# The product with w_out one step further behind the up products of a fused convolution and maxout FFN

## The chip, the cores and the metric

The kernel runs on one core of one Trainium2 chip. The metric is the time on the device in microseconds (us). Five engines work in parallel, each through its own list of instructions in order: TensorE (PE in the profile, its weight loads PEld), VectorE (DVE), ScalarE (ACT), GpSimd (POOL) and SyncE (SP, which issues DMAs here).

## The reference

Two blocks follow each other. The first is a long convolution by FFT with a filter that a small MLP makes, gated by x; the second is a maxout FFN with three up products.

```python
# x, v: (4, 12544, 128); pos_emb: (12544, 64)
h_filt = (np.maximum(pos_emb @ w1, 0.0) @ w2) * np.exp(-0.01 * pos)[:, None]
u = x * v
y = np.fft.irfft(np.fft.rfft(u, n=2 * S, axis=1) * np.fft.rfft(h_filt, n=2 * S, axis=0)[None],
                 n=2 * S, axis=1)[:, :S, :]
t = (x * y).reshape(50176, 128)
h = np.maximum(np.maximum(t @ moe_w1, t @ moe_w2), t @ moe_w3)   # d_ff = 768
out = h @ moe_w_out
```

## The kernel before

**The FFN.** Work goes by tiles of 392 tokens: 32 tiles in each of four batches, and six blocks f of 128 hidden channels in each tile. w1 was subtracted from w2 and w3 beforehand and w1 @ w_out folded into one matrix lin, so that a block needs only two up products: `up` (L674) makes `pa` with four matmuls, ScalarE takes the ReLU into `hid` (L679), four matmuls make `pb`, and VectorE takes the maximum of `hid` and `pb` (L682). `down` (L685) adds the block's product with w_out to the tile's sum in PSUM, the tile `ops`. With the first block it also adds lin times the tile, and with the last one ScalarE copies the sum to `ot` (L695) and GpSimd issues the DMA to the output (L697). All matmuls of `pa`, `pb`, `ops` and `yps` are recorded at L154, the helper `halves_mm`; they are told apart by tile.

**The tile's input.** `t_load` (L619) fetches the convolution's third-stage result `zt` from a scratch in HBM and the tile of x. `t_sums` (L643) makes the sum and the difference of its two halves: on GpSimd (L647, L648) in the first batch and in the first half of the others, on VectorE with a sign (L651) otherwise. `t_last` (L655) does the last stage of the inverse transform, 32 small matmuls into `yps`, and VectorE multiplies it with x into `gt` (L669).

**What runs beside it.** The FFN of batches 0, 1 and 2 shares the engines with the convolution of the next batch. `conv_steps` (L572) spreads that over the 192 steps (32 tiles x 6 blocks) of a batch, by a schedule written out by hand. First come the first-stage transforms `u_first` (L399: L408 on TensorE, L417 on ScalarE, L419 on VectorE). In the second half of a batch come pairs of frequencies: `g_quarter` (L452: L462, L472 on TensorE into `psq`), `g_fold` (L484 on ScalarE, two L487 on VectorE), `q_swap` (L502, L503, twice each, on ScalarE), `q_re` (L507), `q_im` (L512 on VectorE, L515 on GpSimd), `q_unfold` (two L520 on VectorE) and `g_store` (L495, a DMA from GpSimd).

**The order.** Each engine executes its instructions in the order in which the program issues them. The loop at L1015 issues, in step (tile, f): loads and, at f = 1, the sums of the next tile; `up` of this step; `down` of an earlier step; at f = 3 `t_last` of the next tile; then the convolution's work of this step. In the last tile of a batch the sums and `t_last` stand one or two steps later. After 96 tiles the loop ends with the first `up` of the last batch (L1048) and what is left of `down`; the last batch runs in another loop, without a convolution beside it, and products of its own (L742).

**The buffers.** `hid` has three (the default of `up`), the PSUM pool `hps` for `pa` and `pb` together three, which are taken in turn; `yps`, `ps1` and `psq` share two (`cps`), and `ops` has one.

```python
h = up((b, i), f)
if late is not None:
    down(*late)
late = ((b, i), f, h)
```

Of the kernel before, what the change touches and what calls it, by code (L numbers as in the profile page):

```python
# [89 lines left out]
def kernel(  # L90
# [59 lines left out]
    def halves_mm(out, lhsT, rhs, start, stop):  # L150


        for h in range(2):
            nc.tensor.matmul(out[64 * h:64 * h + 64], lhsT[:, 64 * h:64 * h + 64], rhs,  # L154
                             start=start, stop=stop, skip_group_check=True)
# [416 lines left out]
    def conv_steps(b, done):  # L572


        out = []

        def at(slot, late, fn, *args):
            out.append((slot, late, len(out), fn, args))

        per_pair = 170 / (NK + LATE + 0.6 * (NU - done))
        for u in range(done, NU):
            s = (u - done) * 0.6 * per_pair + 9
            at(max(0, int(s) - 9), 0, u_load, b, u)
            at(int(s) - 6, 0, u_mul, u)
            at(int(s) - 5, 0, u_planes, u)
            at(int(s) - 4, 0, u_dma, u)
            at(int(s), 0, u_join, u)
            at(int(s + 1), 1, u_first, u)  # L590
        s0 = int((NU - done - 1) * 0.6 * per_pair + 9) + 6
        for x in range(NK + LATE):
            s = s0 + int(x * per_pair)
            g, z = x if x < NK else None, x - LATE if x >= LATE else None
            at(s, 1, g_quarter, g, z)
            at(s + 1, 0, g_fold, g, z)
            at(s - 4, 0, w_load, x)
            if z is not None:
                at(s + 3, 0, g_store, b, z)
            if g is None:  # L600
                continue
            if g % 2 == 0:
                at(s - 4, 0, q_load, g, min(2, NK - g))
                at(s - 1, 0, h_load, g, min(2, NK - g))
            at(s + 2, 0, q_swap, g)
            at(s + 3, 0, q_re, g)
            at(s + 4, 0, q_im, g)
            at(s + 6, 0, q_unfold, g)
        slots = {}
        for s, _, _, fn, args in sorted(out, key=lambda r: r[:3]):  # L610
            slots.setdefault(s, []).append((fn, args))
        return slots
# [6 lines left out]
    def t_load(b, i):  # L619
        zt = hp.tile([N1, 2, 512], FP32, tag="zt", name="zt", bufs=2)  # L620
        for c in range(2):
            if b == 0:
                nc.sync.dma_start(
                    zt[NK * c:NK * c + NK],
                    zd[b].rearrange("(g a) c t f -> g a c t f", a=2)[
                        :, :, c, 2 * i:2 * i + 2, :].rearrange("g a t f -> g a (t f)"))
                continue
            q, j = divmod(i, NT // 2)
            for a in range(2):
                nc.sync.dma_start(  # L630
                    zt[NK * c:NK * c + NK, a].rearrange("g (t f) -> g t f", t=2),
                    zd[b].rearrange("(g a) c t q f -> g a c t q f", a=2)[
                        :, a, c ^ (a & q), 2 * j:2 * j + 2, q, :])
        zts[b, i] = zt[:, 0], zt[:, 1]
        if i % 2:
            return
        xT = hp.tile([D, 2, 4, NB], FP32, tag="xT", name="xT", bufs=2)
        for c in range(GC):
            nc.sync.dma_start(xT[c * NG:(c + 1) * NG].rearrange("d i p n -> d (i p) n"),
                              x[:, 4 * i:4 * i + 8, c, b, :])  # L640
        xTs[b, i], xTs[b, i + 1] = xT[:, 0], xT[:, 1]

    def t_sums(i, eng=nc.gpsimd):  # L643
        z0, z1 = zts[i]
        even = hp.tile([N1, 512], FP32, tag="even", name="even", bufs=2)
        if i[0] == 0 or i[1] < NT // 2:
            eng.tensor_tensor(out=even[:], in0=z0, in1=z1, op=ALU.add)  # L647
            eng.tensor_tensor(out=z1, in0=z0, in1=z1, op=ALU.subtract)  # L648
        else:
            for out, op in ((even[:], ALU.add), (z1, ALU.subtract)):  # L650
                nc.vector.scalar_tensor_tensor(out=out, in0=z1, scalar=sign_t[:, 0:1], in1=z0,  # L651
                                               op0=ALU.mult, op1=op)
        zts[i] = even[:], z1

    def t_last(i):  # L655
        zt = zts.pop(i)
        ps = cps.tile([P, state["yps"]], FP32, tag="cv", name="yps")
        own = i[0] == B - 1 and i[1] > 1
        g = (lp if own else hp).tile([D, 4, NB], FP32, tag="g", name="gt", bufs=4 if own else 3)
        y = ps[:, 0:N].rearrange("d (p n) -> d p n", p=4)  # L660

        h = NB // 2
        for s in range(4):
            for a in range(2):
                halves_mm(y[:, s, a * h:a * h + h], zt[a][:, s * D:(s + 1) * D],
                          f4p[:, i[0] > 0 and i[1] >= NT // 2, a, :], s == 0 and a == 0, True)
        y = y.rearrange("d p (a m) -> d p m a", a=2)
        xT = xTs.pop(i)
        nc.vector.tensor_tensor(out=g[:].rearrange("d p (m a) -> d p m a", a=2), in0=y,  # L669
                                in1=xT.rearrange("d p (m a) -> d p m a", a=2),  # L670
                                op=ALU.mult)
        gs[i] = g

    def up(i, f, tag="hid", bufs=3):  # L674
        rhs = gs[i][:].rearrange("d p n -> d (p n)")
        h = (lp if tag[0] == "h" and tag != "hid" else hp).tile([P, N], FP32, tag=tag, name="hid", bufs=bufs)
        pa = hps.tile([P, 512], FP32, tag="hps", name="pa")
        halves_mm(pa[:, 0:N], w_sb[1][:, f * P:(f + 1) * P], rhs, True, True)
        nc.scalar.activation(h[:], pa[:, 0:N], Relu)  # L679
        pb = hps.tile([P, 512], FP32, tag="hps", name="pb")  # L680
        halves_mm(pb[:, 0:N], w_sb[2][:, f * P:(f + 1) * P], rhs, True, True)
        nc.vector.tensor_tensor(out=h[:], in0=h[:], in1=pb[:, 0:N], op=ALU.max)  # L682
        return h

    def down(i, f, h):  # L685
        if f == 0:
            pos_[i] = ops.tile([D, 512], FP32, tag="ops", name="ops")
            halves_mm(pos_[i][:, 0:N], lin[:], gs[i][:].rearrange("d p n -> d (p n)"), True,
                      False)
        halves_mm(pos_[i][:, 0:N], wo_sb[:, f, :], h[:], False, f == NF - 1)  # L690
        if f < NF - 1:
            return
        gs.pop(i)
        o = op_.tile([D, 4, NB], FP32, tag="o", name="ot")
        nc.scalar.copy(o[:].rearrange("d p n -> d (p n)"), pos_.pop(i)[:, 0:N])  # L695
        dst = outT.rearrange("d (p b n) -> d p b n", b=B, n=NB)[:, 4 * i[1]:4 * i[1] + 4, i[0], :]
        nc.gpsimd.dma_start(dst, o[:])  # L697
# [94 lines left out]
    def run(steps):  # L792
        for fn, args in steps:
            fn(*args)
# [216 lines left out]

    tiles = [(b, i) for b in range(B) for i in range(NT)]
    LAST = (B - 1) * NT
    late = None
    for n, (b, i) in enumerate(tiles[:LAST]):  # L1015
        if i == 0:
            beside = {}
            beside = conv_steps(b + 1, EARLY if b == 0 else 0)
        if n == 0:
            t_load(*tiles[0])  # L1020
            t_load(*tiles[1])
            t_sums(tiles[0], nc.vector)
            t_last(tiles[0])
        for f in range(NF):

            if i < NT - 2:
                if f == 0:
                    t_load(*tiles[n + 2])
            elif i == NT - 1 and f < 2 and n + 1 + f < len(tiles):
                t_load(*tiles[n + 1 + f])  # L1030
            turn_ = i == NT - 1
            if f == (3 if turn_ else 1):
                t_sums(tiles[n + 1], nc.vector if turn_ else nc.gpsimd)
            if f == 4 and n + 1 == LAST:
                t_sums(tiles[n + 2], nc.vector)
            h = up((b, i), f)
            if late is not None:
                down(*late)
            late = ((b, i), f, h)
            if f == (4 if turn_ else 3):  # L1040
                t_last(tiles[n + 1])
            if f == 5 and n + 1 == LAST:
                t_last(tiles[n + 2])
            s = i * NF + f
            run(beside.pop(s, ()))
            if s == NT * NF - 1:
                assert not beside, sorted(beside)
    first = up((B - 1, 0), 0)  # L1048
    down(*late)
    conv.close()  # L1050


# [20 lines left out]
    step, b = 0, B - 1  # L1073
    for i in range(0, NT, 2):
        h = {}
# [63 lines left out]
```

## Time and profile before

The median of three runs is 2386.82 us (2385.32 to 2388.51). The profiled execution spans 2387.4 us, at a mean granted TensorE clock of 0.993.

| engine | busy us | share of the span | instructions |
|---|---|---|---|
| TensorE | 2318.9 | 97% | 27853 |
| its weight loads | 1367.3 | 57% | 27853 |
| VectorE | 1514.4 | 63% | 2798 |
| ScalarE | 1165.6 | 49% | 2124 |
| GpSimd | 976.0 | 41% | 1153 |

The changed loop runs from about 336 us (first matmul into `ops`) to 1961 us. In a line of a group, the engine and the operation are followed by the tiles written and read, the shapes and the count, then busy us and mean ns of one instruction, and after the bar the idle time of the engine just before these instructions, with what ended most of it. A line of the timeline gives start, duration, engine, line, operation, tiles and, in brackets, the idle time before it and its releaser. The ends of matmuls are modelled: the 0.83 us shown for a group of four run 0.17 us into the next group, which starts 0.66 us after it. A line of the table by stretches gives the stretch, its length, then busy us and count of TensorE, weight loads, VectorE, ScalarE and GpSimd, the granted clock, the share of time that the DMA engines were busy, and GB/s.

### The profile page before, as it was taken

How to read it: one execution, taken by the hardware profiler on the slowest of the kernel's cores; microseconds unless marked ns; L12 is line 12 of the kernel's file. 1: busy time of each engine (PE TensorE's matmuls, PEld its weight loads, DVE VectorE, ACT ScalarE, POOL GpSimd, SP SyncE). 2: the span in 40 equal slices, each digit the busy share in tenths (PEclk: the TensorE clock that was granted, in tenths of full speed). 3: DMA queues.
4: the chain of work that ended last, by engine and by line, in shares of the span. 5: the costliest groups of instructions: out<-in, count | busy, mean ns of one | idle time of the engine just before them, and what ended most of it. 6: DMA issues, size and time to landing. Idle time of an engine off the chain costs nothing.

```text
span 2387.4 us, 67988 instructions
## 1 busy us (share of the span) xinstructions
PE 2318.9 (97%) x27853; PEld 1367.3 (57%) x27853; DVE 1514.4 (63%) x2798; ACT 1165.6 (49%) x2124; POOL 976.0 (41%) x1153
## 2 busy tenths in 40 slices
PE   8999989999999999999999999999999999999998
PEld 7989856654444446654444446654444445666665
DVE  5578857756666647756777747756777755444543
ACT  2688844456556524446565524445556532222222
POOL 1045423334444434424333324434233315666666
PEclk9999999999999999999999999999999999999999
DMA  6878959798988669969889849969989832222221
GB/s 153 200 211 268 285 145 190 151 205 223 221 227 215 172 130 191 186 148 248 207 223 242 201 111 194 184 141 238 223 214 239 222 90 57 69 53 57 71 57 22
DMA packets 473145, 410.92 MB, mean 172 GB/s; under 512 B 328004, under 2 KB 374231, under 8 KB 472834
## 3 DMA queue, kind: packets, MB, share of 16 engines
q1 hardware_dynamic: 433504, 317.61, 60.0%
q0 software_dynamic: 26400, 75.72, 11.0%
q10 hardware_dynamic: 12930, 13.25, 1.7%
q8 instruction: 219, 3.59, 0.7%
q14 instruction: 92, 0.75, 0.1%
HBM read 262.77 MB, written 84.67 MB: 146 GB/s over the span
## 4 chain that ended last, share of the span: by engine, by line
PE 79%; ACT 6%; DVE 6%; DMA 4%; issue 4%; ACTq 0%; POOL 0%; SPq 0%; DVEq 0%; POOLq 0%
PE pa L154 19%; PE pb L154 18%; PE ops L154 16%; PE ops L742 6%; PE ps L408 5%; PE yps L154 5%; PE psq L462 3%; PE ps L163 3%; PE psq L472 2%; DVE cb L487 2%; ACT xs L503 1%; ACT xs L502 1%; DMA hd<-ht 1%; ACT ht L934 1%; DVE hid L682 1%
## 5 line engine op out<-in xcount | busy, mean ns | idle before, releaser
L682 DVE TENSOR_TENSOR hid<-hid,pb 128x392 f32<-128x392 f32 x768 | 428.0, 557 | 564.1 <-PE pb L154 295.7
L679 ACT ACTIVATE hid<-pa 128x392 f32<-128x392 f32 x768 | 383.9, 500 | 640.6 <-PE pa L154 624.9
L154 PE MATMUL pb<-gt,w_sb 128*64 128x392 f32 x3072 | 641.4, 495 | 7.8 <-ACT hid L679 7.8
L154 PE MATMUL pa<-gt,w_sb 128*64 128x392 f32 x3072 | 648.1, 499 | 0.8 <-DVE gt L669 0.8
L154 PE MATMUL ops<-hid,wo_sb 128*64 128x392 f32 x2304 | 481.9, 496 | 30.8 <-DVE hid L682 29.9
L154 PEld LDWEIGHTS pb<-gt,w_sb 128*64 128x64 f32 x3072 | 218.4, 137 | 305.1 <-issue 250.8
L515 POOL TENSOR_TENSOR cb<-cb,xs 128x512 f32<-128x512 f32 x135 | 174.5, 1293 | 466.5 <-DVE xs L512 229.3
L154 PEld LDWEIGHTS ops<-hid,wo_sb 128*64 128x64 f32 x2304 | 160.9, 136 | 261.1 <-issue 147.4
L154 PEld LDWEIGHTS pa<-gt,w_sb 128*64 128x64 f32 x3072 | 196.2, 137 | 137.8 <-issue 93.2
L502 ACT ACTIVATE xs<-cb 32x512 f32<-32x512 f32 x270 | 169.4, 628 | 205.7 <-DVE cb L487 203.2
L697 POOL DMA_DIRECT2D out_dram<-ot x96 | 74.7, 778 | 435.9 <-ACT ot L695 344.1
L419 DVE TENSOR_TENSOR spec<-ps,high 128x360 f32<-128x360 f32 (+1 forms) x204 | 141.9, 737 | 117.2 <-ACT high L417 116.9
L487 DVE TENSOR_TENSOR cb<-psq,eo 128x512 f32<-128x512 f32 (+1 forms) x288 | 174.6, 646 | 0.0
L503 ACT COPY xs<-cb 32x512 f32<-32x512 f32 x270 | 166.2, 616 | 3.2
L417 ACT COPY high<-ps 128x360 f32<-128x360 f32 (+1 forms) x102 | 77.3, 762 | 170.9 <-PE ps L408 113.3
L408 PEld LDWEIGHTS ps<-f1q,uT 98*64 98x64 f32 x3072 | 132.4, 137 | 34.7 <-issue 31.8
L154 PEld LDWEIGHTS yps<-f4p,even 90*64 90x64 f32 x2048 | 117.7, 140 | 41.7 <-issue 36.5
L408 PE MATMUL ps<-f1q,uT 98*64 98x90 f32 x3072 | 137.0, 241 | 3.1 <-DVE spec L419 2.6
L154 PE MATMUL yps<-f4p,even 90*64 90x49 f32 x2048 | 127.2, 222 | 3.5 <-DMA f4p<-f4p_const 3.5
L154 PE MATMUL yps<-f4p,zt 90*64 90x49 f32 x2048 | 128.8, 224 | 0.1
L669 DVE TENSOR_TENSOR gt<-yps,xT 128x392 f32<-128x392 f32 x128 | 72.1, 563 | 84.5 <-PE yps L154 42.3
L520 DVE TENSOR_TENSOR xs<-cb 128x256 f32<-128x256 f32 x270 | 120.4, 487 | 0.0
(130 smaller groups left out, 3336.1 us busy)
## 6 DMA issues: line engine op xcount, KB each, us to landing
ht<-hd SPq DMA_DIRECT2D x264, 256.0 KB, 5.8
wt<-wq_const SPq DMA_DIRECT2D x144, 256.0 KB, 6.4
zd<-cb POOLq DMA_DIRECT2D x135, 256.0 KB, 5.6
zt<-zd SPq DMA_DIRECT2D x384, 90.0 KB, 3.1
sq<-spec SPq DMA_DIRECT2D x264, 128.0 KB, 6.8
ut<-in_xr_dram SPq DMA_DIRECT2D x128, 196.0 KB, 4.1
ut<-in_vr_dram SPq DMA_DIRECT2D x128, 196.0 KB, 4.3
xT<-in_x_dram SPq DMA_DIRECT2D x256, 98.0 KB, 3.7
```

Source lines behind the costliest of these rows:

```text
L154: nc.tensor.matmul(out[64 * h:64 * h + 64], lhsT[:, 64 * h:64 * h + 64], rhs, start=start, stop=stop, skip_group_check=True)
L408: nc.tensor.matmul(ps[64 * c:64 * c + 64, 256 * i + h * N1:256 * i + (h + 1) * N1], t[:, 2 * ((at + i) % 8) + h].rearrange("n r t -> n (r ...
L417: nc.scalar.copy(high, v[:, 0])
L419: nc.vector.tensor_tensor(out=spec[:, :, a, at:at + n], in0=v[:, 1], in1=high, op=op)
L487: nc.vector.tensor_tensor(out=cb[:, a, lo:hi], in0=ps[:, lo:hi], in1=eo[:, lo:hi], op=op)
L502: nc.scalar.mul(xs[at:at + 32], xt[at + 32:at + 64], -1.0)
L503: nc.scalar.copy(xs[at + 32:at + 64], xt[at:at + 32])
L515: nc.gpsimd.tensor_tensor(out=xts[g], in0=xts[g], in1=xs[:], op=ALU.add)
L520: nc.vector.tensor_tensor(out=ab[:, q], in0=y[:, 0], in1=y[:, 1], op=op)
L679: nc.scalar.activation(h[:], pa[:, 0:N], Relu)
L682: nc.vector.tensor_tensor(out=h[:], in0=h[:], in1=pb[:, 0:N], op=ALU.max)
L742: nc.tensor.matmul(ps[64 * c:64 * c + 64, 0:H2], w, rhs[:, H2 * c:H2 * c + H2], start=start, stop=True, skip_group_check=True)
```

## The change

In the loop over the first three batches `down` lags two steps behind `up` in place of one: the maximum of a block is made two steps before TensorE multiplies it with w_out. It is meant to give VectorE more time to make that maximum before TensorE needs it. The last two downs follow the first `up` of the last batch. The number of buffers and every instruction stay as they are.

```diff
-    late = None
+    late = []
     for n, (b, i) in enumerate(tiles[:LAST]):
...
             h = up((b, i), f)
-            if late is not None:
-                down(*late)
-            late = ((b, i), f, h)
+            late.append(((b, i), f, h))
+            if len(late) > 2:
+                down(*late.pop(0))
             if f == (4 if turn_ else 3):
                 t_last(tiles[n + 1])
...
     first = up((B - 1, 0), 0)
-    down(*late)
+    for l in late:
+        down(*l)
     conv.close()
```

## The prediction

> **What bounds the kernel now.** I read the page first. TensorE is busy 97% of 2387.4 us, VectorE 63%, ScalarE 49%, and the granted clock is 0.99, so the kernel can gain only where TensorE stands still. The groups of instructions say where (busy and mean ns | idle before, and what ended it):
>
> ```profile
> L154 PE MATMUL pb<-gt,w_sb 128*64 128x392 f32 x3072 | 641.4, 495 | 7.8 <-ACT hid L679 7.8
> L154 PE MATMUL ops<-hid,wo_sb 128*64 128x392 f32 x2304 | 481.9, 496 | 30.8 <-DVE hid L682 29.9
> ```
>
> The product with w_out (down, tile ops) carries 30.8 us of TensorE's idle time, nearly all of it a wait for the max of L682; the second up product (pb) carries 7.8 us, a wait for the ReLU of L679. The waits of TensorE alone give counts and the longest single wait:
>
> ```profile
> PE ops L154 <- DVE hid L682: 29.9, 28, 2.0
> PE pb L154 <- ACT hid L679: 7.8, 11, 3.7
> ```
>
> Only 28 of the 576 downs in question are late, by about 1.07 us each. The longest pb wait, 3.73 us at 1967.09, stands outside the changed loop's steady part. The table by stretches (first columns: stretch, length, TensorE busy) shows where the rest lies:
>
> ```profile
> 536.00:830.00 294.00, 284.99 (x3096) 141.95 (x3094) 194.95 (x356) 173.99 (x317) 135.80 (x131) 0.99 0.84 215
> 830.00:1075.00 245.00, 245.00 (x2774) 138.16 (x2770) 151.40 (x264) 103.55 (x190) 90.15 (x113) 1.00 0.84 162
> 1075.00:1380.00 305.00, 292.01 (x3204) 140.53 (x3204) 219.12 (x405) 180.34 (x330) 103.04 (x107) 1.00 0.89 221
> 1620.00:1925.00 305.00, 292.06 (x3200) 140.14 (x3194) 217.85 (x401) 181.55 (x332) 103.71 (x108) 1.00 0.91 222
> ```
>
> While the first half of a batch runs (830 to 1075) TensorE never stops. It stops where g_quarter, g_fold and q_swap run beside the FFN: 9.0 us in the first such stretch, 13.0 and 12.9 us in the next two. That is the whole prize, 34.9 us, and about 0.2 us more for each wait (below). The timeline of TensorE shows one late down, which recurs nearly alike eight times (1132, 1185, 1271, 1323 and again in the last stretch):
>
> ```profile
> 1130.02 0.83 PE L154 MATMUL pb<-gt,w_sb 128*64 128x392 f32 x4
> 1132.31 0.88 PE L154 MATMUL ops<-hid,wo_sb 128*64 128x392 f32 x4 [1.47 <-DVE hid L682]
> 1133.12 0.67 PE L462 MATMUL psq<-sq,wt 64*64 64x128 f32 x16
> ...
> 1134.15 0.88 PE L154 MATMUL pa<-gt,w_sb 128*64 128x392 f32 x4
> 1134.86 0.83 PE L154 MATMUL pb<-gt,w_sb 128*64 128x392 f32 x4
> ```
>
> From pb's start to that of the down pass 2.29 us, where 0.66 is usual (1129.36 to 1130.02): 1.63 us lost, with 1.47 recorded as idle, and the group behind starts 0.15 us later than usual (0.81 after the down), elsewhere 0.05. VectorE and ScalarE at the same place:
>
> ```profile
> 1131.70 0.55 DVE L682 TENSOR_TENSOR hid<-hid,pb 128x392 f32<-128x392 f32 x1
> ```
> ```profile
> 1130.44 0.63 ACT L502 ACTIVATE xs<-cb 32x512 f32<-32x512 f32 x1 [1.89 <-DVE cb L487]
> ...
> 1132.34 0.61 ACT L503 COPY xs<-cb 32x512 f32<-32x512 f32 x1
> 1132.98 0.50 ACT L679 ACTIVATE hid<-pa 128x392 f32<-128x392 f32 x1
> ```
>
> The max comes late because L520, L507, L487 and the two L651 stand ahead of it in VectorE's order; the next ReLU comes late because four swaps stand ahead of it on ScalarE. The first is what the change attacks. The second is not touched.
>
> **What the Trainium skill says.** "TensorE: Matmul & The Clock Gate", Part 3, The mechanism: matmuls start and end in program order. The trace agrees: during the 1.47 us the queued L462 does not overtake. So what counts is what stands ahead of which wait. "Perfetto Trace Analysis", Optimization Strategy: the same gap repeating on the engine that should be saturated can mean too few buffers. The trace half agrees: the gaps repeat, and the pb waits are such a wait for a PSUM buffer. "SBUF — State Buffer", Who interferes with whom: a VectorE instruction with two SBUF inputs and a GpSimd one that reads SBUF exclude each other. The trace agrees: two L520, 0.75 us together at 1127.79, take 3.58 us beside the sums of L647 and L648:
>
> ```profile
> 572.04 3.58 DVE L520 TENSOR_TENSOR xs<-cb 128x256 f32<-128x256 f32 x2
> ```
> ```profile
> 571.12 0.79 POOL L697 DMA_DIRECT2D out_dram<-ot  x1 [1.33 <-ACT ot L695]
> 571.91 0.71 POOL L495 DMA_DIRECT2D zd<-cb  x1
> 572.51 1.40 POOL L647 TENSOR_TENSOR even<-zt 90x512 f32<-90x512 f32 x1
> ```
>
> **The change, part by part.** No instruction is added or removed; every down moves one step later in TensorE's order.
>
> The hid buffers. Three exist, and with the longer lag three are live: the ReLU of step n overwrites the buffer that down(n-3) read. On TensorE down(n-3) now stands just ahead of pa(n), and the ReLU must wait for pa(n) anyway. Cost 0, hidden by pa (0.66 us).
>
> The wait for the max. hps has three buffers in turn, so pa(n+2) needs the buffer that max(n) frees, and pb(n+1) the one that ReLU(n) frees. Until now down(n) met max(n) first. Now pa(n+2) does, later by one down (0.66 us) and the convolution's matmuls of that step (0 to 2 us). The late max is then mostly covered. The pb wait keeps its place, and TensorE reaches it sooner: this decides what is left of the prize.
>
> Site kind B, the one shown, eight times. After pb (1130.02 + 0.66) TensorE does the older down until 1131.34, then L462 and L472 (1.03 us, from 1133.12 to 1134.15) until 1132.37; max is done at 1132.25, so pa runs at 1132.37 instead of 1134.15. Then pb must wait for the ReLU, which ends at 1133.48: it starts at about 1133.53 instead of 1134.86, and pays about 0.2 us of restart. Net 1.1 us of the 1.47. The 0.46 us pb wait that follows some 11 us later (1143.54) hangs on a chain that itself starts from TensorE's yps, so it moves along and stays. 8 x 1.1 = 8.8 us.
>
> Site kind C (1.15 us at 1089.30, six times). The same walk: the next ReLU ends only at 1091.92, behind four swaps, and pb started at 1091.97 already. Net 0, between -0.2 and +0.5 each.
>
> Small downs (0.08 to 0.57 us, 2.3 us over the two last stretches): half kept, 1.1 us.
>
> Site kind A (1.95 us, four times in the first stretch, each with one of 0.30). The walk at 577.94 gives: pa could run at 578.45, but the ReLU ends at 580.55, so pb starts at 580.60 instead of 581.41, net 0.6 us after the restart; the ScalarE-bound stretch behind it (swaps until 594.01 and 602.74) then takes about as much back. Net 0, between -0.4 and +0.6.
>
> Moved along: the copy ot (L695) and the output DMA (L697), with their down. On GpSimd L697 waits for ot, and the sums of L647/L648 queue behind it. With the longer lag the last down of a tile falls into step 1 of the next, and the sums are issued ahead of that step's down: they no longer queue behind L697. Here 1.33 us of idle and 0.79 us of L697 go from ahead of them, and they start about 2 us earlier, beside L507 and L682 instead of two L520. Of the 2.83 us of exclusion (3.58 - 0.75) I expect about 1.3 us to remain, so 1.5 us less on VectorE. That chain (L520, L512, L487, swaps, ReLU) is what then binds pb, so some 0.6 us of it counts, between -0.5 and 1.2. Four sites: 2.4 us. What queues behind L697 in its new place, L515 and the stores, has 4 to 7 us of idle before it at these sites.
>
> The end of the loop. Before the first up of the last batch one down fewer has been done, and two follow it in place of one. The last down, its copy, the output DMA and the ReLU that waited for it until 1966.54 come at the same distance: 0. The last stretch, from 1961 us on, is unchanged: 0.
>
> Sum: 8.8 + 0 + 1.1 + 0 + 2.4 = 12.3 us, less about 1.3 us for new short ReLU waits where TensorE had been late enough to see none: 11 us. 2386.8 - 11 = 2375.8 us.
>
> **The rivals.** *All late downs are covered and nothing takes their place*: 29.9 us and 28 restarts of 0.2 us, so 35 us, 2352 us. For it speaks that VectorE and ScalarE are busy only 72% and 60% in the worst stretches; against it the walks above, in which a ReLU bounds pb three times out of three. *The wait moves one for one* from the max to the ReLU: 2386 us, no change. For it speaks kind C; against it kind B, where 1.3 us lie between the ReLU's end and the old pb. *Slower*: the sums, now earlier on GpSimd, meet L507, L512 or L520 in tiles where they met nothing. Some 15 tiles of the first convolution stretch can each lose up to 1.3 us of VectorE (one L647), 20 us; if three quarters of it shows on TensorE, 15 us, less the 9.9 us of B and the small downs, that is +5 us, 2392 us. Against it: VectorE is busy only 66% there, and the worst overlap exists already.
>
> **How the numbers follow.** My forecast, a gain of about 5 to 17 us: 0.76; all covered: 0.07; one for one: 0.12; slower: 0.05. The low end takes B at 1.4, C at 0.4, A with the sums at 1.2 and the small downs in full: 11.2 + 2.4 + 4.8 = 18 us, 2368.5. The high end takes B at 0.7 and nothing else, with A at -0.4: 5.6 - 1.6 = 4 us, 2383. Faster by over 0.2% (4.8 us): 0.82; within: 0.13; slower: 0.05.
>
> **What would show it.** After the change the idle time ahead of ops should fall from 30.8 to under 3 us, and that ahead of pb rise from 7.8 to 20 to 30 us with ACT hid L679 as releaser; pa should hardly wait for DVE hid L682. TensorE's idle time in the three stretches should fall from 34.9 to about 25 us, in the last two most. The two L520 of kind A should take less than 3.58 us. Wrong would be: pa waits for the max (slack too small), ReLU waiting for ops (hid buffers too few), or pb idle growing by as much as ops idle falls.

## The result and the profile after

The changed kernel takes 2375.54 us (median; 2374.38 to 2377.9) beside 2386.09 us for the kernel before (2385.32 to 2388.51): a ratio of 0.9955 [0.9938, 0.9973]. That is a gain of 10.6 us, where 11 were forecast. The number is right; the experiments show that the sum behind it isn't. One term of it was too small by some 9 us, and losses of some 7 us were put at nothing.

The groups of instructions of the changed kernel, for the same two groups (busy us and mean ns | idle before, and what ended it):

```profile
L154 PE MATMUL pb<-gt,w_sb 128*64 128x392 f32 x3072 | 644.9, 497 | 33.3 <-ACT hid L679 33.3
L154 PE MATMUL ops<-hid,wo_sb 128*64 128x392 f32 x2304 | 478.5, 492 | 0.0
```

The down no longer waits at all, and the second up product waits 33.3 us for the ReLU, where it waited 7.8. Together 38.6 us of idle time became 33.3. That is half of the gain; the other half shows as TensorE's busy time, which fell from 2318.9 to 2312.2 us with the same 27853 instructions. A part of that is the clock (next section), the rest was not followed. The waits of TensorE give the count:

```profile
PE pb L154 <- ACT hid L679: 33.3, 53, 3.7
```

There were 11 such waits before; now there are 53. No wait of `pa` for the max shows (its 0.8 us belongs to `gt`). The same four stretches as before (first columns: stretch, length, TensorE busy; the last is shifted by 10 us, since the program is ahead by then):

```profile
536.00:830.00 294.00, 288.75 (x3160) 142.58 (x3158) 192.06 (x366) 177.64 (x325) 138.61 (x135) 1.00 0.90 220
830.00:1075.00 245.00, 243.65 (x2762) 138.20 (x2760) 146.08 (x258) 103.83 (x188) 87.03 (x113) 1.00 0.84 163
1075.00:1380.00 305.00, 294.55 (x3266) 144.98 (x3264) 221.03 (x414) 180.75 (x332) 102.93 (x107) 1.00 0.90 219
1610.00:1915.00 305.00, 294.73 (x3268) 145.10 (x3264) 221.40 (x412) 183.40 (x336) 104.25 (x108) 1.00 0.92 223
```

TensorE's idle time is 5.25, 10.45 and 10.27 us in the first, third and fourth row: 26.0 us in place of 34.9. And the stretch in which it never stopped now has 1.35 us of idle time. The site of kind B that the prediction walked through, on TensorE:

```profile
1125.97 0.83 PE L154 MATMUL pb<-gt,w_sb 128*64 128x392 f32 x4
1126.63 0.83 PE L154 MATMUL ops<-gt,lin 128*64 128x392 f32 x4
1127.29 0.83 PE L154 MATMUL ops<-hid,wo_sb 128*64 128x392 f32 x4
...
1129.08 0.88 PE L154 MATMUL pa<-gt,w_sb 128*64 128x392 f32 x4
1130.15 0.88 PE L154 MATMUL pb<-gt,w_sb 128*64 128x392 f32 x4 [0.19 <-ACT hid L679]
```

and on VectorE and ScalarE:

```profile
1128.32 0.55 DVE L682 TENSOR_TENSOR hid<-hid,pb 128x392 f32<-128x392 f32 x1
```
```profile
1128.96 0.61 ACT L503 COPY xs<-cb 32x512 f32<-32x512 f32 x1
1129.60 0.91 ACT L679 ACTIVATE hid<-pa 128x392 f32<-128x392 f32 x2
```

The max of the first `pb` ends at 1128.87, later than the down behind that `pb` starts (1127.29). It makes nobody wait now, because that down uses an older block. What binds the next `pb` is the first of the two ReLUs at 1129.60, which had to wait for four swaps on ScalarE. From `pb` to `pb` it is 4.18 us here with 0.66 us of a lin product in between, so 3.52; before it was 4.84 (1130.02 to 1134.86). The gain is 1.32 us, and the walk gave 1.33 before the restart.

### The profile page after: what moved, and what is told of

It is laid out like the page before. It is cut to its first block, busy times and chain, and to the rows that moved or that the text cites. A ratio compares the mean times of both kernels' runs of the same rounds, so it can differ in the third digit from the quotient of the medians.

```text
span 2376.1 us, 68062 instructions
## 1 busy us (share of the span) xinstructions
PE 2312.2 (97%) x27853; PEld 1372.2 (58%) x27853; DVE 1489.2 (63%) x2798; ACT 1165.4 (49%) x2124; POOL 968.7 (41%) x1153
## 3 DMA queue, kind: packets, MB, share of 16 engines
q8 instruction: 219, 3.59, 0.7%
## 4 chain that ended last, share of the span: by engine, by line
PE 78%; ACT 8%; DMA 5%; DVE 4%; issue 3%; ACTq 0%; POOL 0%; SPq 0%; DVEq 0%; POOLq 0%
PE pb L154 19%; PE pa L154 19%; PE ops L154 16%; PE ops L742 6%; PE ps L408 5%; PE yps L154 5%; PE ps L163 3%; PE psq L462 2%; ACT xs L503 2%; ACT xs L502 2%; DMA hd<-ht 2%; DVE cb L487 2%; PE psq L472 2%; ACT hid L679 1%; ACT ht L934 1%
## 5 line engine op out<-in xcount | busy, mean ns | idle before, releaser
L154 PE MATMUL pb<-gt,w_sb 128*64 128x392 f32 x3072 | 644.9, 497 | 33.3 <-ACT hid L679 33.3
L154 PEld LDWEIGHTS ops<-hid,wo_sb 128*64 128x64 f32 x2304 | 168.8, 137 | 210.4 <-issue 210.4
L697 POOL DMA_DIRECT2D out_dram<-ot x96 | 75.1, 783 | 323.1 <-ACT ot L695 285.5
L503 ACT COPY xs<-cb 32x512 f32<-32x512 f32 x270 | 166.2, 616 | 3.1
L377 POOL COPY planes<-ut 128x784 uint16<-128x784 uint16 x90 | 75.9, 843 | 135.6 <-DVE ut L356 135.4
```

Source lines behind the costliest of these rows:

```text
L377: nc.gpsimd.tensor_copy(pl_[:, :, :, 0:NB], a[:].bitcast(U16).rearrange("p s (n h) -> p h s n", h=2))
L503: nc.scalar.copy(xs[at + 32:at + 64], xt[at:at + 32])
```

## Where the time went, stretch by stretch

One mark recurs in every kernel: the start of the ReLU of the first block of a tile. From the differences between such marks comes the gain of each stretch against the kernel before, in us. "(1, 10)" is tile 10 of batch 1; the columns are the changed kernel and three of the experiments below.

| from – to | time before | changed kernel | output DMA later, lag 1 | lag 2, PSUM in strict turn | and swaps split |
|---|---|---|---|---|---|
| (0, 0) – (0, 10) | 170.1 | -2.30 | -0.89 | +0.67 | +0.41 |
| (0, 10) – (0, 30) | 336.2 | +7.45 | +8.39 | +7.44 | +15.68 |
| (0, 30) – (1, 10) | 201.9 | -2.00 | -0.01 | -0.34 | -0.35 |
| (1, 10) – (1, 30) | 343.7 | +6.36 | +1.93 | +5.64 | +17.09 |
| (1, 30) – (2, 10) | 201.9 | -1.96 | -0.01 | -0.37 | -0.36 |
| (2, 10) – (2, 30) | 344.3 | +7.18 | +2.24 | +7.19 | +15.62 |
| (2, 30) – end | 455.8 | -1.52 | -0.12 | -1.10 | -0.87 |
| sum | | 13.21 | 11.53 | 19.13 | 47.22 |

The profiled span fell by 11.3 us (2387.4 to 2376.1). The remaining 1.9 us of the 13.2 lie ahead of the loop: the profiled run of the changed kernel reached the first mark at 335.45 us and that of the kernel before at 333.53, with the same program up to there. Over all runs that mark lies between 331.2 and 335.9 us, so differences of one or two microseconds between single spans mean nothing. Differences between marks inside the loop do mean something, where the clock is the same.

It isn't the same everywhere. In the kernel before, two stretches of 3.41 us, from 646.0 and from 782.5 us, have half the clock. They follow two of the four longest late downs; behind the other two, with a wait just as long, the clock stayed full. On TensorE, and in the table by stretches (the number ahead of the last two is the granted clock):

```profile
577.94 0.88 PE L154 MATMUL ops<-hid,wo_sb 128*64 128x392 f32 x4 [1.95 <-DVE hid L682]
578.65 0.27 PE L154 MATMUL yps<-f4p,even 90*64 90x49 f32 x4
...
645.59 1.23 PE L154 MATMUL ops<-hid,wo_sb 128*64 128x392 f32 x4 [1.95 <-DVE hid L682]
646.60 0.41 PE L154 MATMUL yps<-f4p,even 90*64 90x49 f32 x4
```
```profile
577.90:581.30 3.40, 3.36 (x72) 2.51 (x74) 0.71 (x2) 2.59 (x5) 0.50 (x1) 1.00 0.51 148
646.00:649.40 3.40, 3.40 (x56) 2.90 (x56) 1.16 (x3) 2.15 (x4) 0.05 (x1) 0.50 1.01 216
```

The two tiles concerned (18 and 26) take 18.96 and 18.98 us, two like them with a full clock (14 and 22) 17.85: 1.1 us each. The other three kernels of the table have no such stretch between 340 and 1920 us, so 2.2 us of each gain in the second row come from the clock in this one profile. That the long waits bring it on is likely, but not shown.

The table shows a sum that the forecast did not have: +21.0 us in the three worked stretches, and -7.8 us at the three starts of batches and at the end.

## The experiments

Every kernel computes the whole output. Each was timed beside the kernel before (2387.95 us in the first set, 2388.69 and 2388.48 in the later ones).

### Only the output DMA later, lag one

The forecast gave the moved output DMA 2.4 us and the lag the rest. This kernel keeps the lag of one and issues the DMA (L697) one step later, so that on GpSimd the sums stand ahead of it exactly as in the changed kernel.

```diff
-        nc.gpsimd.dma_start(dst, o[:])
+        outs.append(lambda: nc.gpsimd.dma_start(dst, o[:]))
...
             h = up((b, i), f)
+            ready, outs[:] = outs[:], []
             if late is not None:
                 down(*late)
+            for o_ in ready:
+                o_()
```

> The kernel before (lag of one step), with one thing moved: the output DMA (L697) is issued one step later, behind the sums of the next tile, as the changed kernel has it on GpSimd; the downs stay. Theory: part of the gain is this move on GpSimd and has nothing to do with the lag. The sums then no longer meet two L520, the longest late downs (1.95 us) go or shrink, TensorE's idle time ahead of ops falls from 30.8 to about 22 to 26 us, nearly all in the stretch 536 to 830, and the time is 3 to 7 us below the kernel before. Rival (only the lag matters): ops keeps 30 us and the time is within 1 us of before.

Measured: 2375.48 us (2374.64 to 2379.42), ratio 0.9946 [0.9934, 0.9959], so 12.5 us less than before, more than the 3 to 7 expected and as much as the whole change. TensorE's waits in this kernel:

```profile
PE ops L154 <- DVE hid L682: 23.0, 26, 1.5
PE pb L154 <- ACT hid L679: 7.4, 9, 3.7
```

The waits for the max are nearly all still there (26 of 28), but they are shorter. The gain therefore isn't that of the lag. A site of kind A in the changed kernel, where GpSimd's order is the same, shows what happens, first GpSimd, then VectorE:

```profile
574.27 1.38 POOL L647 TENSOR_TENSOR even<-zt 90x512 f32<-90x512 f32 x1
575.72 1.61 POOL L648 TENSOR_TENSOR zt<-zt 90x512 f32<-90x512 f32 x1
577.28 0.79 POOL L697 DMA_DIRECT2D out_dram<-ot  x1
```
```profile
574.88 1.32 DVE L507 TENSOR_TENSOR cb<-cb,ht 128x512 f32<-128x512 f32 x1
576.60 1.36 DVE L520 TENSOR_TENSOR xs<-cb 128x256 f32<-128x256 f32 x2
```

The sums no longer stand behind a DMA that waits for its copy. They meet L507 (1.32 us, 0.68 when alone) and the two L520 (1.36) instead of the two L520 alone (3.58). In the lag-one kernel of this experiment L520 and L507 take 1.35 + 1.33 = 2.68 us at the same site, where it took 3.58 + 0.68 = 4.26: VectorE saves 1.58 us, and the forecast said 1.5. But the late down at that site shrinks from 1.95 to 0.38 us, by all of the 1.58, and not by "some 0.6", and so do the three others. In this kernel:

```profile
575.64 0.88 PE L154 MATMUL ops<-hid,wo_sb 128*64 128x392 f32 x4 [0.38 <-DVE hid L682]
```

In marks the four sites yield +1.57, +2.84, +0.75 and +2.86 us, 8.0 together. The second and the fourth hold the two stretches at half clock, 1.1 us each; the third has a new late down of 0.72 us behind it (722.57). 4.2 us more come in the two later stretches, most of it in tile 12, where the sums are still on GpSimd and the forecast counted nothing for this part.

### The sums put behind the output DMA again, lag two

The counterpart: the changed kernel with the sums issued behind the down of step 1, and so behind the output DMA again.

```diff
-            if f == (3 if turn_ else 1):
-                t_sums(tiles[n + 1], nc.vector if turn_ else nc.gpsimd)
+            if turn_ and f == 3:
+                t_sums(tiles[n + 1], nc.vector)
...
                 down(*late.pop(0))
+            if not turn_ and f == 1:
+                t_sums(tiles[n + 1], nc.gpsimd)
```

> The changed kernel (lag of two), but the sums on GpSimd are issued behind the down of step 1 and so behind the output DMA, in the relative order of the kernel before. Theory: the lag alone is left. Ops idle stays at 0 and pb idle at about 33 us or more; the first stretch loses most of its gain, the two later ones keep about 5 us each: 2379 to 2382 us, 3 to 6 us over the changed kernel. Rival (only the lag matters): the time of the changed kernel, 2375 to 2376 us.

Measured: 2396.93 us, ratio 1.0032 [1.002, 1.0043]: 21 us slower than the changed kernel and 9 slower than before, which is a miss. This is not a clean undoing. With a lag of two that DMA itself stands a step later, so the sums come later than in either kernel: in tile 14 of batch 0 the first of them starts 2.90 us after the mark, where it was 1.58 before and 0.40 in the changed kernel. TensorE's waits show something that neither has:

```profile
PE pb L154 <- ACT hid L679: 37.5, 66, 3.7
PE psq L462 <- issue: 10.4, 12, 1.8
```

Twelve stops of 10.4 us ahead of L462, whose releaser isn't recorded, and 4.2 us more for the ReLU. The two L520 are longer again in sum (112.5 us, 106.9 in the changed kernel), and L507 takes 1.76 us at 558.36 beside L648. The stops and the ReLU make 14.6 us of the 21. The profile also has three stretches of 3.41 us at half clock, from 562.6, 699.2 and 835.7 us. Tile 13 of batch 0, which holds one, loses 3.90 us against the kernel before, tile 17 with the same stop and a full clock 2.54; so an estimate for the three is some 4 us. The rest was not followed. What it supports: at a lag of two, the place of the sums on GpSimd decides the sign of the change. What it can't say is how much of the first experiment's gain is less exclusion and how much is sums that are ready earlier.

### The PSUM buffers in strict turn

The changed kernel loses 2 us at each start of a batch. The timeline of TensorE at the start of batch 1's FFN shows it:

```profile
876.76 0.83 PE L154 MATMUL pa<-gt,w_sb 128*64 128x392 f32 x4
878.18 0.88 PE L154 MATMUL pb<-gt,w_sb 128*64 128x392 f32 x4 [0.60 <-ACT hid L679]
...
880.97 0.88 PE L154 MATMUL pb<-gt,w_sb 128*64 128x392 f32 x4 [0.60 <-ACT hid L679]
```
```profile
877.63 0.50 ACT L679 ACTIVATE hid<-pa 128x392 f32<-128x392 f32 x1 [1.48 <-PE pa L154]
```

`pb` waits for the ReLU that reads the `pa` just in front of it. So it was given the buffer of its own step's `pa`, although the description of the kernel and the forecast took the three buffers to be used in turn. Why the pool chose so was not followed. In this kernel each `pa` and `pb` has its place written down.

```diff
-        pa = hps.tile([P, 512], FP32, tag="hps", name="pa")
+        pa = hps.tile([P, 512], FP32, tag=f"hps{state['hps'] % 3}", name="pa")
...
-        pb = hps.tile([P, 512], FP32, tag="hps", name="pb")
+        pb = hps.tile([P, 512], FP32, tag=f"hps{(state['hps'] + 1) % 3}", name="pb")
+        state['hps'] += 2
```

> The changed kernel, with the three PSUM buffers of pa and pb taken in strict turn (three buffers of their own, by a counter) in place of the pool's own choice. In the changed kernel pb of tile 1 of a batch waits in steps 0 and 1 for the ReLU of its own step (0.60 us each at 878 and 881), because the pool handed it the buffer just read. Theory: these waits go, with about 0.2 us of restart each, in three batches: 4 to 5 us below the changed kernel, 2371 us. Rival (the waits only move to the next step, or the pool's choice is as good): 2375 to 2376 us.

Measured: 2369.73 us, ratio 0.9918 [0.9904, 0.9931], 5.8 us less than the changed kernel. In TensorE's waits, six short ones have gone:

```profile
PE pb L154 <- ACT hid L679: 29.8, 47, 3.8
```

Six waits of 0.60 us, two for each of the three batches, are the 3.5 us of difference to 33.3; each also delays what follows it, so that from `pa` to `pb` it was 1.42 us in place of 0.66, or 4.6 us for the six. The marks agree: tile 1 of each batch loses 1.63 or 1.64 us in the changed kernel, 4.9 together, and 0.00 in this one, and the starts of batches 1 and 2 lose 0.34 and 0.37 us in all in place of 2.00 and 1.96.

### Four hid buffers, and a lag of three

The forecast costed the three hid buffers at nothing. Two kernels take them up: the changed one with four, and one with four and a lag of three.

```diff
-    def up(i, f, tag="hid", bufs=3):
+    def up(i, f, tag="hid", bufs=4):
```

> The changed kernel with four hid buffers in place of three. Theory: the ReLU never waits for the down that frees its hid buffer, since that down stands ahead of pa on TensorE: within 2 us of the changed kernel. Rival (three buffers are one too few for a lag of two): 3 us or more faster, with pb idle falling.

Measured: 2374.6 us, ratio 0.9939 [0.9926, 0.9951], within 1 us of the changed kernel, with 33.0 us of waits ahead of `pb` in place of 33.3. The hid buffers bind nothing.

```diff
+    def up(i, f, tag="hid", bufs=4):
...
-            if len(late) > 2:
+            if len(late) > 3:
```

> The changed kernel with a lag of three steps and four hid buffers. Theory: with a lag of two no down waits any longer, and pb's wait for the ReLU sets the pace, which a longer lag does not touch: ops idle 0, pb idle about 33 us, no gain over the changed kernel; some waits of pa for the max may appear, since the step's down no longer lies where it did, so 0 to 10 us slower. Rival (the max is still what holds TensorE up): faster by another 5 us or more, with pb idle falling.

Measured: 2385.6 us, ratio 0.9991 [0.9984, 0.9997], so 10 us slower than a lag of two. Its waits on TensorE:

```profile
PE pb L154 <- ACT hid L679: 37.0, 54, 3.4
...
PE pa L154 <- DVE hid L682: 3.5, 8, 0.4
```

`pa` does reach the buffer that the max frees too early, eight times, and the ReLU binds 3.7 us longer. That is 7.2 of the 10 us; the other 3 stay open. One down still stands between `up` and `up` in each step, only an older one, so why these waits come was not followed either. More lag wasn't more slack here.

### The swaps split in two

If the ReLU behind four swaps takes what the lag offers, then a shorter block should set the rest free. Here the four ScalarE instructions of `q_swap` go out in two pairs in successive steps, and `q_re` one step later.

```diff
-            at(s + 2, 0, q_swap, g)
-            at(s + 3, 0, q_re, g)
+            at(s + 2, 0, q_swap, g, 0)
+            at(s + 3, 0, q_swap, g, 64)
+            at(s + 4, 0, q_re, g)
             at(s + 4, 0, q_im, g)
```

> The changed kernel, with q_swap's four ScalarE instructions (2.5 us in a row ahead of a ReLU) issued as two and two in successive steps, and q_re one step later. Nothing else moves. Theory: what holds pb after the change is a ReLU that stands behind four swaps; with at most two ahead of it (1.25 us) it comes in time. TensorE's idle time ahead of pb falls from 33 to under 10 us (3.7 us at the loop's end stay), and the time falls by 15 to 30 us below the changed kernel, 2345 to 2360 us. Rival (VectorE's chain L520, L512, L487 is what makes the ReLU late, the swaps only pass it on): pb idle 25 us or more, within 5 us of the changed kernel.

Measured: 2343.74 us, ratio 0.981 [0.9797, 0.9824], 32 us less than the changed kernel and a little more than expected. The lines of this kernel stand one lower (the ReLU is L680, the swaps L503 and L504). TensorE's wait and ScalarE's timeline at one site:

```profile
PE pb L154 <- ACT hid L680: 7.4, 7, 3.8
```
```profile
1086.14 0.63 ACT L503 ACTIVATE xs<-cb 32x512 f32<-32x512 f32 x1 [1.01 <-DVE cb L487]
1086.78 0.62 ACT L504 COPY xs<-cb 32x512 f32<-32x512 f32 x1
1087.42 0.50 ACT L680 ACTIVATE hid<-pa 128x392 f32<-128x392 f32 x1
1087.94 0.63 ACT L503 ACTIVATE xs<-cb 32x512 f32<-32x512 f32 x1
```

The ReLU runs between two pairs of swaps. Of 53 waits seven are left: the 3.8 us at the end of the loop and the six at the starts of batches. The later `q_re` belongs to this edit and to the two kernels that follow; it was not tried by itself.

The same edit in the kernel before:

> The same split of the swaps in the kernel before (lag of one). Theory: the late downs wait for VectorE, which the swaps do not touch, so most of ops' 30 us stays and only pb's few waits go: 0 to 8 us below the kernel before, 2379 to 2387 us. Lag and split then are worth much more together than apart. Rival (the ScalarE order is all that matters, the lag is not needed): as fast as the split with the lag of two.

Measured: 2376.62 us, ratio 0.9949 [0.9936, 0.9963], 12 us less than before, a little more than expected. The downs' wait for the max rises there to 35.1 us (36 times), and with 4.3 us ahead of `pb` the two waits together are 1.7 us longer than before. So where the 12 us come from isn't seen in them; some 2.2 us can be the clock, which has no stretch at half in this profile between 340 and 1950 us. Its order on GpSimd is still that of the kernel before, so it can't be set beside the split at lag two for the lag's worth. The next kernel evens that out.

### Lag one with GpSimd's new order and the swaps split

The edit is that of the first experiment together with the split, so that against the kernel with the swaps split and lag two, only the lag is different.

> Lag of one, with the output DMA one step later and the swaps split: all that the fastest kernels have, apart from the lag and the strict turn of the PSUM buffers. It prices the lag where no ReLU hides it. Theory: VectorE's late max holds the downs as before, ops idle 28 to 35 us, pb idle about 4 us; 2368 to 2376 us, so that the lag is worth 25 to 32 us once the ReLU is in time. Rival (GpSimd's order and the swaps do the work, the lag adds little, as it adds little in the changed kernel): under 2352 us.

Measured: 2372.4 us, ratio 0.9933 [0.992, 0.9947]. TensorE's waits (the max is L683 here):

```profile
PE ops L154 <- DVE hid L683: 31.4, 34, 1.8
PE pb L154 <- ACT hid L680: 3.7, 1, 3.7
```

So the waits for the max are the limit here, and those for the ReLU in the steady loop are gone. In medians, us:

| GpSimd's order as in the changed kernel | lag 1 | lag 2 | the lag gains |
|---|---|---|---|
| swaps in one block | 2375.48 | 2375.54 | 0 |
| the same, at lag 2 with PSUM in strict turn (not run at lag 1) | 2375.48 | 2369.73 | 5.8, both edits |
| swaps split | 2372.4 | 2343.74 | 28.7 |
| the split gains (first row to third) | 3.1 | 31.8 | |

The two waits stand one behind the other: the lag alone gains nothing, the split alone 3.1 us, both together 31.7 us. The kernels were timed in four sets, in which the kernel before took 2386.09 to 2388.69 us, so differences of 2 or 3 us between them are no result; the 28.7 and the 31.8 are.

### The best of both

> The changed kernel with the split swaps and with the PSUM buffers of pa and pb in strict turn. Theory: both effects add, 5 to 6 us below the kernel with the split swaps alone. Rival: with the ReLU early enough the pool's choice costs nothing, so the same time as with the split alone.

The split swaps and the strict turn together, at lag two: 2341.5 us, ratio 0.9801 [0.9787, 0.9814], 47 us less than before. In the stretch of the first batch TensorE doesn't stop:

```profile
536.00:830.00 294.00, 294.00 (x3240) 148.41 (x3238) 205.07 (x374) 181.28 (x331) 140.42 (x138) 1.00 0.89 219
```

Ahead of `pb` only the 3.7 us at the end of the loop remain. The strict turn brings 2.2 us here, with overlapping ranges (2338.45 to 2343.23 beside 2341.85 to 2344.81), where 5 to 6 were expected. The six waits have gone. The profile has one stop that the split kernel's hasn't, 1.11 us ahead of L462 at 1735.63, for the max; beyond this, why the time fell by less than 4.6 us was not settled.

## Why the prediction was right, and where it was not

**The main mechanism: right.** The wait for the max disappears and a wait for the ReLU takes most of its place. Idle time ahead of `ops` under 3 us: it is 0.0. Ahead of `pb` 20 to 30: it is 33.3, of which 3.5 are the six waits at starts of batches that were not foreseen. `pa` waits for the max: never.

**Kind B: right. Kind C: right for the lag.** B gains 1.32 us at the site shown, 1.1 predicted. Over the two tiles that hold it the lag gains 0.99, since a `pb` wait of 0.85 us follows at 1145.08 that was not there before. The eight sites come to 7.1 us in this way (marks, changed kernel less first experiment), 8.8 predicted; the difference of 1.7 is such new waits, for which the forecast took off 1.3. For C, the site in tile 12 of batch 1 has a `pb` wait of 1.12 us behind it (1088.93) in place of the late down of 1.15. Tiles 12 and 13 gain 1.59 us in the changed kernel and as much in the lag-one kernel with the same order on GpSimd, so this comes from the sums and not from the lag; tiles 20 and 21, with the next such site, gain 0 in both. In each of the two later stretches the lag alone gives +4.43 and +4.94 us.

**Kind A: right for the lag, wrong for the sums.** The lag alone gives -0.94 us in the first stretch, 0 predicted. The step that failed is "some 0.6 us of it counts … Four sites: 2.4 us". The saving on VectorE was sized well (1.58 us beside 1.5), but all of it came off the late down, four times: the four tiles take 16.28 us each at a lag of one and 16.27 to 16.28 at a lag of two, where they took 17.85, and 18.96 and 18.98 with the slow clock. The order also helped outside these four sites. The term measures 11.5 us in marks, of which 2.2 are the two stretches at half clock: it was short by 9, or by 7 without the clock. The prediction took the ReLU at the end of the same chain for what then binds `pb`, and so let only a part count; in the changed kernel no `pb` waits in these four tiles.

**The starts of the batches and the end of the loop: put at nothing, -6.75 us.** In marks (changed kernel less first experiment) the starts of the three batches give -1.41, -1.99 and -1.95, and the loop's end -1.40. (The first of them also holds the slow groups of the last section.) The choice of PSUM buffers makes 4.9 us of it. The step that failed is "hps has three buffers in turn", which holds in the steady loop only.

At the loop's end 0.66 us are a matter of the mark, for one more down is pending when it is taken (the first row has the counterpart). The rest goes with the clock: at half it runs for 3.41 us in the kernel before and in the first experiment, for 6.83 us in the changed kernel, and not at all in the profile of the changed kernel with four hid buffers, whose last row is +0.97 where the changed kernel has -1.52. So the forecast's 0 for this part is not contradicted.

**The sum.** The forecast's 12.3 - 1.3 = 11 us became 11.5 from the order on GpSimd, +8.4 from the lag in the three worked stretches and -6.75 at the starts and the end: 13.2 us in marks. The order was put at 2.4, the lag at 9.9 - 1.3 = 8.6, and the starts and the end at nothing. So the lag was sized rightly where it was walked through, and two errors of +9.1 and -6.75 us nearly cancelled: that the number came out right is luck in this part. And with the same GpSimd order the lag as a whole is worth nothing in the medians (2375.54 beside 2375.48). The low end of the range has a slip: it names the small downs in full, but its 11.2 + 2.4 + 4.8 us leave out their 2.3.

**The signs.** "From 34.9 to about 25 us, in the last two most" was half right: 26.0 us in sum, but the first stretch gave most (9.0 to 5.25), the others 13.0 to 10.45 and 12.9 to 10.27. That was the sign of the mis-sized sums.

**The rivals.** *All covered* was 2352 us. With the ReLU in time the lag is worth 28.7 us, beside the 35 of this rival, so what stood in its way was the swaps; that the kernel then goes below 2352 us (2343.7) is owed to the order on GpSimd as well. *One for one* fails on the idle times (30.8 us went, 25.5 came), but it is what the lag comes to in the medians once its new waits at the starts of batches are counted. *Slower* did not come: the sums, now earlier, lengthened L507 (93.7 to 97.3 us in sum), but L520 became shorter by more (120.4 to 106.9).

## What to carry to other kernels

Before one slackens a wait, look at which engine's order binds next at the same place; here the lag gained 0 us with four swaps in one block and 28.7 with two pairs, and only the pair of edits paid. And follow every instruction that moves along with the one that is meant: the place of a moved output DMA on GpSimd, which let two sums pass a DMA that waits for its copy, was worth more than the lag in this kernel. Where an order of buffers is part of the argument, check it at the turns of the loop and not only in its steady part.

## What the runs showed of the hardware that was not expected

**An exclusion shows as a longer instruction.** VectorE's time for the two L520 is 3.58 us beside GpSimd's sums and 0.75 alone, and no idle time is recorded for it. "SBUF — State Buffer", Who interferes with whom, which the prediction used, names the two kinds of instruction; the runs agree, and also that L507 goes from 0.68 to 1.32 us. VectorE's busy time fell from 1514.4 to 1489.2 us with not one instruction less; L520 and L507 together make 9.9 us of this, the rest was not followed.

**A slow TensorE behind a long wait.** The first groups of the loop, in the changed kernel's timeline of TensorE, start 1.33 and 1.31 us apart in place of 0.66:

```profile
333.79 1.58 PE L154 MATMUL pa<-gt,w_sb 128*64 128x392 f32 x4 [0.75 <-DVE gt L669]
335.12 1.55 PE L154 MATMUL pb<-gt,w_sb 128*64 128x392 f32 x4
```

This goes on until 339.04, for four groups, and in the kernel before for three (331.87 to 335.60). Until 331.67, 2.1 us earlier, TensorE had waited 3.59 us for a constant. "TensorE: Matmul & The Clock Gate", Part 1, What's actually happening, says that the clock is halved after an idle window of about 3.4 us, and that the windows run free, so that the number of slow groups differs from run to run. The trace agrees: a granted clock of 0.55 between 333 and 340 us, a doubled distance, and two to five slow groups in five of the traces. Over the usual 0.66 us a group they cost 1.4 to 2.9 us in these five, so the scatter alone is 1.5 us. In one thing the measurement differs from that page: in the kernel before the clock also fell to half behind an idle time of only 1.95 us (645.59), much shorter than the page's window, and behind the same idle time at 577.94 it did not.
